# Gated mix of linear attention and a squared-relu MLP: matmul operands at other byte offsets, and gate logits formed on VectorE

## The chip, the core and the metric

One NeuronCore of a Trainium2 chip runs the whole kernel in one launch. The metric is the device time in microseconds (us) of that core; the kernel before takes 442.57 us (median of three runs, 442.34 to 442.65). The engines are called as in the profile: PE is TensorE's matmul side, PEld its weight load, DVE is VectorE, ACT is ScalarE, POOL is GpSimd, and SP issues most of the DMAs.

## The reference

The input is x with 2048 rows and 448 columns. The result is a gate between a linear-attention block (16 heads of 28) and a two-layer perceptron of width 1792:

```python
g = _sigmoid((x * gate_w).sum(-1, keepdims=True))
a = _A_ref(x, A_wqkv, A_wo)
b = _B_ref(x, B_w1, B_b1, B_w2, B_b2)
return g * a + (1 - g) * b
```

In `_A_ref`, `phi(t) = where(t > 0, t + 1, exp(t)) + 1e-6` is taken of queries and keys, `kv = phi(k)^T v` and the sum of `phi(k)` are formed for each head over all rows, and the output is `phi(q) kv / (phi(q) . sum)` times `wo`. In `_B_ref` the hidden layer is `relu(x w1 + b1)` squared, times `w2`, plus `b2`. The gate needs one number for each row, the logit `sum(x * gate_w)`.

## The kernel before

**Precision.** Every fp32 operand is split into a rounded part and a remainder, both in TensorE's fp32r format. A product then takes three matmuls (high by high, high by low, low by high). The 448-wide contraction is laid out as four chunks of 128, the last of which holds its 64 rows twice, so that it needs two matmuls: 11 matmuls for each contraction over x, 12 for four tiles of the second layer.

**Tiles.** Rows go in four blocks of 512 (`NB`), each of four tiles of 128. PSUM tiles are one bank each. The matmuls of this program have four widths. The names are those of the profile:

- `h_ps` (hidden layer, L213) and `q_ps` (queries, L77): 512 columns stream. The stationary operand is a 128-column piece of `w1` or `wq_s`; the moving one is `xh` or `xl`, 512 rows of x.
- `o_ps` (second layer, L242), `g_ps` (x^T phi(k), L77) and `a_ps` (attention output, L77): 448 columns stream, out of `w2`, `ph`/`pl` and `m_s`. The stationary operand is a piece of `hh`/`hl`, `nh`/`nl` or `qh`/`ql`.
- `k_ps` (keys, L77): 450 columns stream out of `wk_s`. Its last two columns are `gate_w` twice, so that column 448 of the PSUM tile is the gate logit, which L280 copies into `logit`.
- `m_ps` (kv by wo, 12 matmuls of 448), `d_ps` (denominators, 8 of 512), and a few small ones.

**Counts.** 56 hidden tiles of 11 make 616 `h_ps` matmuls; 4 blocks of 40 make 160 `q_ps`; 56 steps of 12 make 672 `o_ps`; `a_ps` and `k_ps` have 16 groups of 11 and `g_ps` four times 12, 12, 12 and 8, so 176 matmuls each.

**Addresses.** The pools place a tile by its size, so pads in the code set the byte offset within a partition. Taken modulo 256, the program as built has these starts, where every step between chunks and column pieces is a multiple of 256 and keeps them:

| matmuls | stationary start | moving start |
|---|---|---|
| `h_ps`, `q_ps` | 0 | 0 |
| `o_ps`, `a_ps`, `g_ps`, `k_ps` | 0 | 64 |
| `m_ps`, `d_ps` | 0 | 0 |

**Order.** The order of the work is the order of the code, apart from what the framework's scheduler swaps between neighbours on an engine. In the first phase a step of the loop runs `up` (11 matmuls), `down` of the step before (12) and then `keys` of one tile (11) or a `gram` (11 or 8). What the other engines do with a PSUM tile stands in `after()` of `keys`, which the next `run_todo()` issues: ACT takes the exponential, DVE forms `r` (L261) and `p` (L262, into `r`), ACT rounds it to `ph`, DVE takes the remainder `pl` (L65), POOL adds to `ksum` (L286) and splits the row tile `xnr` (L65). `gram` of the same block reads `ph`, `pl`, `nh` and `nl`. Block 0 is the tightest place: `gram(0, 0)` is issued right after the keys of tile 3. Loads go through SP's queue in order (L51) into 15 shared slots.

The second phase runs the other half of the hidden layer, queries, denominators and attention, from about 225 us on.

Of the kernel before, what the change touches and what calls it, by code (L numbers as in the profile page):

```python
# [7 lines left out]
F = mybir.dt.float32  # L8
# [19 lines left out]


@with_exitstack  # L30
def gated_mix_kernel(ctx: ExitStack, tc: tile.TileContext, xt, xn, wk, wq, wv, wo, w1a, w1b, w2, b1, b2, hmask,
                     kvmask, halves, out):
    nc = tc.nc
    act, dve, pool, pe, sp = nc.scalar, nc.vector, nc.gpsimd, nc.tensor, nc.sync

    keep = ctx.enter_context(tc.tile_pool(name="keep", bufs=1))


    rest = ctx.enter_context(tc.tile_pool(name="rest", bufs=1, side="right"))
# [10 lines left out]
    def load(dst, src):  # L50
        sp.dma_start(out=dst, in_=src)  # L51
# [74 lines left out]

    def split_w1(h, g, c, hi_eng=act):
        if c == 0:
            n = (TB, 3 * P)[g]
            w = keep.tile([P, 7 * n + (16, 0)[g]], R, name=f"w1_{h}{g}", tag=f"w1{g}", bufs=1)  # L130
            w1_s[h, g] = w[:, :7 * n].rearrange("p (c n) -> p c n", c=7)
        split_w(w1_s[h, g], c, w1_raw.pop((h, g, c)), hi_eng, dve)

    w2_s, w2_raw = {}, {}
# [16 lines left out]
    wk_raw = {}  # L151

    def load_wk(c):
        wk_raw[c] = slot([P, D + 2], F, f"wkr{c}")
        load(wk_raw[c], wk[c])

    warm = keep.tile([P, 400], mybir.dt.bfloat16, name="warm")[:, :256]  # L160
    dve.memset(warm, 0.0)
    warm_ps = acc_p.tile([P, 512], F, name="warm_ps", tag="acc")
    for _ in range(18):
# [24 lines left out]
        load_wk(c)  # L188

    b2_s = keep.tile([P, D], F, name="b2_s")  # L190
    hm = keep.tile([P, P], R, name="hm")
    dve.memset(ones, 1.0)
    ksum = keep.tile([P, D], F, name="ksum")
    part = [keep.tile([P, D], F, name=f"part{t}") for t in range(NT)]

    phase1 = ExitStack()
    tmp = phase1.enter_context(tc.tile_pool(name="tmp", bufs=1, side="right"))
# [66 lines left out]
    def keys(t):  # L264
        b, i = divmod(t, 4)
        ps = ms_p.tile([P, 512], F, name=f"k_ps{t}", tag="ms")
        products(ps[:, :D + 2], [term for c in range(4)
                                 for term in terms_x(*xs[b], slice(i * P, (i + 1) * P), wk_s, slice(0, D + 2), c)])
        e = slot([P, D], F, f"e{t}")
        r = slot([P, D], F, f"r{t}")  # L270
        p = r
        ph = tmp_p.tile([P, D], R, name=f"ph{t}", tag="ph", bufs=4)
        pl = tmp_p.tile([P, D], R, name=f"pl{t}", tag="pl", bufs=4)

        if t == 0:
            pool.memset(tmp_p.tile([P, 48], F, name="off"), 0.0)

        def after():
            phi(ps[:, :D], e, r, p)
            dve.tensor_copy(logit[:, t:t + 1], ps[:, D:D + 1])  # L280
            split_hi(act, ph, p)
            split_lo(dve, pl, p, ph)
            if t == 0:
                pool.tensor_copy(ksum, p)
            else:
                pool.tensor_tensor(ksum, ksum, p, op=ALU.add)  # L286
            nh = tmp.tile([P, 512], R, name=f"nh{t}", tag="nh", bufs=4)
            nl = tmp.tile([P, 384], R, name=f"nl{t}", tag="nl", bufs=4)
            raw = xn_raw.pop(t)
            split_hi(act, nh[:, :D], raw)  # L290
            split_lo(pool, nl, raw[:, :384], nh[:, :384])
            split_lo(pool, nh[:, D:], raw[:, 384:], nh[:, 384:D])
            pend[t] = (ph, pl, nh, nl)
        return [after]
# [15 lines left out]
                dve.tensor_tensor(gsum[c], ps[:, :D], gsum[c], op=ALU.add)  # L310
        return [after]

    wq_s = keep.tile([P, 7, TB], R, name="wq_s")
    wq_raw = {}

    def load_wq(c):
# [69 lines left out]
    def m_product(j):  # L386
        wh, wl = wo_s.pop(j)
        ps = ms_p.tile([P, 512], F, name=f"m_ps{j}", tag="ms")
        products(ps[:, :D], [(kv[0][:, j], wh), (kv[0][:, j], wl), (kv[1][:, j], wh)])
        m = late.tile([P, 2, D], R, name=f"m{j}", tag="m", bufs=1)  # L390

        def after():
            split_hi(act, m[:, 0], ps[:, :D])
            split_lo(dve, m[:, 1], ps[:, :D], m[:, 0])

            p = j * 32
            for c in range(3):
                pool.dma_start(out=m_s[p:p + 32, c::4, :D][:, :2], in_=m[c * 32:c * 32 + 32])
            pool.dma_start(out=m_s[p:p + 16, 3, :D], in_=m[96:112, 0])
            pool.dma_start(out=m_s[p + 16:p + 32, 3, :D], in_=m[112:, 1])  # L400
        return [after]


# [64 lines left out]
    def attention(b, i):  # L468
        t = 4 * b + i
        cols = slice(i * P, (i + 1) * P)  # L470
        ps = ms_p.tile([P, 512], F, name=f"a_ps{t}", tag="ms")
        terms = []
        for c in range(3):
            h, lo = qs[c]
            terms += [(h[:, cols], m_s[:, c, :D]), (h[:, cols], m_s[:, 4 + c, :D]), (lo[:, cols], m_s[:, c, :D])]
        h, lo = qs[3]
        terms += [(h[:, cols], m_s[:, 3, :D]), (lo[:, cols], m_s[:, 3, :D])]
        products(ps[:, :D], terms)
        u = late.tile([P, D], F, name=f"u{t}", tag="q", bufs=NLATE)
        act.activation(u, ps[:, :D], AF.Copy, scale=gate[:, 0, t:t + 1])  # L480
        dve.scalar_tensor_tensor(part[t], part[t], gate[:, 1, t:t + 1], u, op0=ALU.mult, op1=ALU.add)  # L481
# [26 lines left out]
    for f in range(2, 4):  # L508
        hidden(first[f], 0, f)

    wkm = keep.tile([P, 3632], R, name="wk_s", tag="wkm", bufs=1)
    wk_s = wkm[:, :7 * TB].rearrange("p (c n) -> p c n", c=7)

    load_xn(0)
    load_w2(2)
    load_w2(3)
    for c in range(4):
        split_w(wk_s[:, :, :D + 2], c, wk_raw[c], act, dve)
    down(0, 0)
    load_xn(1)  # L520
    for c in range(4):
        load_w1(0, 1, c)
    todo += keys(0)
    split_w2(2)
    load(b2_s, b2.partition_broadcast(P))
    down(0, 1)
    run_todo()
# [96 lines left out]
    for n, b in enumerate(order):  # L624
        then = order[n + 1] if n + 1 < NB else None
        for f in range(NF - NH, NF):
            fl = f - NH
            run_todo()
            up(b, f)
            if fl:  # L630
                if n + 1 < NB or f + 1 < NF:
                    down(b, f - 1)
            elif n == 0:
                down(b, NH - 1)
                half_done(b)
            else:
                down(order[n - 1], NF - 1)
                for i in range(4):
                    finish(order[n - 1], i)
            if n == 0:  # L640
                if fl < 4:
                    todo += queries(b, (3, 0, 1, 2)[fl])
                if fl == 0:
                    for c in range(4):
                        load_w1(1, 1, c)
                    kv_product()
                    phase1.close()
                    late = ctx.enter_context(tc.tile_pool(name="late", bufs=1, side="right", reuse_waits="tile"))
                    m_s = keep.tile([P, 3632], R, name="m_s", tag="wkm", bufs=1)
                    m_s = m_s[:, :7 * D].rearrange("p (c n) -> p c n", c=7)  # L650
                    for j in range(2):
                        load_wo(j)
                if fl == 1:
                    for c in range(4):
                        split_w1(1, 1, c)
                if fl in (1, 2):
                    for j in range(2 * fl - 2, 2 * fl):
                        split_wo(j)
                        todo += m_product(j)
                    if fl == 1:  # L660
                        for j in range(2, 4):
                            load_wo(j)
                if fl < 2:
                    load_w2(NH + 5 + fl)
                    split_w2(NH + 4 + fl)
                if fl == 2:
                    split_w2(NH + 6)
                if fl == 4:
                    todo += denominators(b)
                if fl == 5:  # L670
                    for c in range(4):
                        scaled(b, c)
                if fl == 6:
                    for i in range(4):
                        attention(b, i)
            else:
                if fl == 0:
                    todo += denominators(b)
                if fl == 1:
                    for c in range(4):  # L680
                        scaled(b, c)
                if 2 <= fl < 6:
                    attention(b, fl - 2)
            if then is not None:
                if fl < 2:
                    load_x(then, 2 * fl)
                    load_x(then, 2 * fl + 1)
                if 1 <= fl < 3:
                    split_x(then, 2 * fl - 2)
                    split_x(then, 2 * fl - 1)  # L690
                if n and 3 <= fl:
                    todo += queries(then, (3, 0, 1, 2)[fl - 3])
                if n == 0 and fl in (5, 6):
                    for c in ((3, 0), (1, 2))[fl - 5]:
                        todo += queries(then, c)
# [56 lines left out]
```

## Time and profile before

| | before |
|---|---|
| median of three runs | 442.57 us |
| the profiled execution | 441.92 us |
| its span, first to last instruction | 440.1 us |
| PE busy | 432.9 us (98%), 2054 matmul records |
| PEld busy | 380.7 us (87%) |
| DVE busy | 268.0 us (61%) |
| ACT busy | 172.7 us (39%) |
| POOL busy | 58.5 us (13%) |
| granted TensorE clock | 1.000 |

A matmul's own duration in the profile runs until its drained end and overlaps the next one. How fast matmuls follow each other is read from stretches of a view: the chain of waits gives start, length and count of each uninterrupted run, and length by count is the time from one start to the next.

### The profile page before, as it was taken

What the parts mean: (1) busy time and instruction counts of PE and PEld (TensorE: products, weight loads), DVE (VectorE), ACT (ScalarE), POOL (GpSimd) and SP (SyncE); (2) the same over time, 40 slices, a digit from 0 to 9 for tenths busy, and PEclk for the clock granted to TensorE, in tenths of its full rate; (3) what the DMA queues carried; (4) which work ended last, traced back from release to release, by engine and by line L of the source; (5) the groups of instructions that cost most, each with busy time, mean ns of one, the idle gap of its engine ahead of it and who ended that gap; (6) DMA issues with size and microseconds to landing.
All of it is one profiled execution on the core that took longest, in us unless ns stands there. A gap on an engine that the chain in (4) does not pass through costs nothing.

```text
span 440.1 us, 5482 instructions
## 1 busy us (share of the span) xinstructions
PE 432.9 (98%) x2054; PEld 380.7 (87%) x2054; DVE 268.0 (61%) x452; ACT 172.7 (39%) x298; POOL 58.5 (13%) x76
## 2 busy tenths in 40 slices
PE   9999999999999999999999989999999999999996
PEld 6798898899888889898988868888888898888895
DVE  5958436552587427573467668788454984549423
ACT  5955235331355114451344334335322453234321
POOL 0233124210252005420002420000000000000000
PEclk9999999999999999999999999999999999999999
DMA  7652201021031210333146311040100501002002
GB/s 264 188 174 69 89 13 57 24 66 47 24 118 31 67 45 1 110 102 82 54 123 151 73 38 24 1 147 33 25 0 0 181 0 26 0 0 85 1 1 83
DMA packets 18315, 28.77 MB, mean 65 GB/s; under 512 B 2880, under 2 KB 12784, under 8 KB 18288
## 3 DMA queue, kind: packets, MB, share of 16 engines
q1 hardware_dynamic: 17072, 26.81, 19.9%
q0 software_dynamic: 1216, 1.61, 1.9%
q8 instruction: 16, 0.26, 0.3%
q14 instruction: 11, 0.09, 0.1%
HBM read 22.09 MB, written 3.67 MB: 59 GB/s over the span
## 4 chain that ended last, share of the span: by engine, by line
PE 91%; DVE 3%; DMA 2%; ACT 2%; issue 1%; SPq 0%; DVEq 0%; ACTq 0%
PE o_ps L242 30%; PE h_ps L213 28%; PE q_ps L77 8%; PE a_ps L77 8%; PE g_ps L77 8%; PE k_ps L77 7%; DMA wkr<-in_wk 1%; DMA xr<-in_xt 1%; PE kv_ps L364 1%; ACT hr L217 1%; PE m_ps L77 1%; DVE wk_s L65 0%; DVE hh L62 0%; DVE r L261 0%; DVE r L262 0%
## 5 line engine op out<-in xcount | busy, mean ns | idle before, releaser
L213 PE MATMUL h_ps<-xh,w 128*128 128x512 f32 x392 | 126.9, 392 | 0.1
L242 PE MATMUL o_ps<-w,hh 128*128 128x448 f32 x448 | 125.5, 363 | 0.7 <-DVE hh L62 0.7
L242 PEld LDWEIGHTS o_ps<-w,hh 128*128 128x128 f32 x448 | 83.8, 188 | 10.2 <-DVE hh L62 1.4
L213 PE MATMUL h_ps<-xl,w 128*128 128x512 f32 x224 | 87.5, 391 | 0.0
L213 PEld LDWEIGHTS h_ps<-xh,w 128*128 128x128 f32 x392 | 73.5, 188 | 15.4 <-ACT xh L58 0.4
L242 PE MATMUL o_ps<-w,hl 128*128 128x448 f32 x224 | 79.6, 363 | 0.0
L217 ACT ACTIVATE hr<-h_ps,b_s 128x512 f32<-128x512 f32 x56 | 38.3, 683 | 96.9 <-PE h_ps L213 89.8
L62 DVE CAST hh<-hr 128x512 fp32r<-128x512 f32 x56 | 25.3, 452 | 40.4 <-ACT hr L218 40.0
L213 PEld LDWEIGHTS h_ps<-xl,w 128*128 128x128 f32 x224 | 42.1, 188 | 8.3 <-DVE xl L65 0.4
L242 PEld LDWEIGHTS o_ps<-w,hl 128*128 128x128 f32 x224 | 42.0, 188 | 2.9 <-DVE hl L65 0.2
L65 DVE TENSOR_TENSOR hl<-hr,hh 128x512 fp32r<-128x512 f32 x56 | 41.1, 734 | 2.2
L218 ACT ACTIVATE hr<-hr 128x512 f32<-128x512 f32 x56 | 35.3, 630 | 1.3
L77 PE MATMUL k_ps<-wk_s,xh 128*128 128x450 f32 x112 | 33.7, 367 | 0.0
L77 PE MATMUL q_ps<-xh,wq_s 128*128 128x512 f32 x100 | 33.0, 390 | 0.0
L77 PE MATMUL a_ps<-m_s,qh 128*128 128x448 f32 x112 | 32.2, 362 | 0.0
L65 POOL TENSOR_TENSOR nl<-xnr,nh 128x384 fp32r<-128x384 f32 x16 | 18.2, 1139 | 94.2 <-ACT nh L58 94.2
L286 POOL TENSOR_TENSOR ksum<-ksum,r 128x448 f32<-128x448 f32 x15 | 19.3, 1284 | 52.1 <-DVE r L262 52.1
L481 DVE SCALAR_TENSOR_TENSOR part<-part,gate,u 128x448 f32<-128x448 f32 x16 | 10.9, 683 | 24.9 <-ACT u L480 24.9
L480 ACT ACTIVATE u<-a_ps,gate 128x448 f32<-128x448 f32 x16 | 10.2, 635 | 37.2 <-PE a_ps L77 37.2
L261 DVE TENSOR_SCALAR r<-k_ps 128x448 f32<-128x448 f32 x16 | 10.0, 623 | 23.7 <-ACT e L260 21.7
L77 PE MATMUL k_ps<-wk_s,xl 128*128 128x450 f32 x64 | 23.6, 369 | 0.0
L77 PE MATMUL g_ps<-pl,nh 128*128 128x448 f32 x64 | 23.3, 364 | 0.3 <-DVE pl L65 0.3
(104 smaller groups left out, 562.0 us busy)
## 6 DMA issues: line engine op xcount, KB each, us to landing
xr<-in_xt SPq DMA_DIRECT2D x27, 256.0 KB, 3.2
xnr<-in_xn SPq DMA_DIRECT2D x16, 224.0 KB, 2.6
out<-out SPq DMA_DIRECT2D x16, 224.0 KB, 2.0
w2r<-in_w SPq DMA_DIRECT2D x14, 224.0 KB, 2.9
w1r<-in_w1a SPq DMA_DIRECT2D x8, 256.0 KB, 2.8
w1r<-in_w1b SPq DMA_DIRECT2D x8, 192.0 KB, 2.9
m_s<-m POOLq DMA_DIRECT2D x12, 112.0 KB, 2.7
wqr<-in_wq SPq DMA_DIRECT2D x4, 256.0 KB, 3.0
```

The costliest lines, as they stand in the source:

```text
L62: eng.tensor_copy(hi, src)
L65: eng.tensor_tensor(lo, src, f32(hi), op=ALU.subtract)
L77: pe.matmul(out_ps, a, b, start=(i == 0), stop=(i == n - 1))
L213: pe.matmul(ps, a, m, start=(c == 0 and n == 0), stop=(c == 3 and n == 1))
L217: act.activation(r, ps, AF.Relu, bias=b1_s[:, f:f + 1])
L218: act.activation(r, r, AF.Square)
L242: pe.matmul(o_ps[i][:, :D], a, m, start=(f % NH == 0 and n == 0), stop=(f % NH == NH - 1 and n == 2))
L261: dve.tensor_scalar(r, ps, 0.0, 1e-6, op0=ALU.max, op1=ALU.add)
L286: pool.tensor_tensor(ksum, ksum, p, op=ALU.add)
L364: pe.matmul(kv_ps[:JE, js], wv_s[c][:, js], gsum[c][:, js], start=(c == 0), stop=(c == 3))
L480: act.activation(u, ps[:, :D], AF.Copy, scale=gate[:, 0, t:t + 1])
L481: dve.scalar_tensor_tensor(part[t], part[t], gate[:, 1, t:t + 1], u, op0=ALU.mult, op1=ALU.add)
```

## The change

- `w1` tiles and `wq_s` get pads ahead of them, so that the stationary operands of `h_ps` and `q_ps` begin at 144 modulo 256. Their moving operands stay at 0.
- The pads of `warm`, `wk_s`, `m_s` and `off` change (the warm-up operand now lies in the first `part` tile), so that the moving operands of `o_ps`, `a_ps`, `g_ps` and `k_ps` begin at 160. Their stationary ones stay at 0. `m_ps` keeps 0 and 0; the stationary operand of the eight `d_ps` matmuls moves to 224.
- `wk_s` loses its two gate columns, so `k_ps` streams 448. The logit of a tile is formed on DVE by one `scalar_tensor_tensor` with an accumulated output, from the row tile `xnr` and a broadcast copy of `gate_w`, `gw_s`, which one more DMA brings. Its elementwise result goes into `e`, which has been read by then.

```diff
@@ -126,9 +127,9 @@
     def split_w1(h, g, c, hi_eng=act):
         if c == 0:
-            n = (TB, 3 * P)[g]
-            w = keep.tile([P, 7 * n + (16, 0)[g]], R, name=f"w1_{h}{g}", tag=f"w1{g}", bufs=1)
-            w1_s[h, g] = w[:, :7 * n].rearrange("p (c n) -> p c n", c=7)
+            n, a, z = ((TB, 36, 4), (3 * P, 60, 0))[g]
+            w = keep.tile([P, a + 7 * n + z], R, name=f"w1_{h}{g}", tag=f"w1{g}", bufs=1)
+            w1_s[h, g] = w[:, a:a + 7 * n].rearrange("p (c n) -> p c n", c=7)
...
-    warm = keep.tile([P, 400], mybir.dt.bfloat16, name="warm")[:, :256]
+    part = [keep.tile([P, D], F, name=f"part{t}") for t in range(NT)]
+    warm = part[0].bitcast(mybir.dt.bfloat16)[:, :256]
...
+    gw_s = keep.tile([P, D], F, name="gw_s")
...
-        products(ps[:, :D + 2], [term for c in range(4)
-                                 for term in terms_x(*xs[b], slice(i * P, (i + 1) * P), wk_s, slice(0, D + 2), c)])
+        products(ps[:, :D], [term for c in range(4)
+                             for term in terms_x(*xs[b], slice(i * P, (i + 1) * P), wk_s, slice(0, D), c)])
...
         if t == 0:
-            pool.memset(tmp_p.tile([P, 48], F, name="off"), 0.0)
+            pool.memset(tmp_p.tile([P, 24], F, name="off"), 0.0)
...
             phi(ps[:, :D], e, r, p)
-            dve.tensor_copy(logit[:, t:t + 1], ps[:, D:D + 1])
             split_hi(act, ph, p)
...
             raw = xn_raw.pop(t)
+            dve.scalar_tensor_tensor(e, raw, 1.0, gw_s, op0=ALU.mult, op1=ALU.mult, accum_out=logit[:, t:t + 1])
             split_hi(act, nh[:, :D], raw)
...
-    wq_s = keep.tile([P, 7, TB], R, name="wq_s")
+    wq_s = keep.tile([P, 44 + 7 * TB + 28], R, name="wq_s")[:, 44:44 + 7 * TB]
+    wq_s = wq_s.rearrange("p (c n) -> p c n", c=7)
...
-    wkm = keep.tile([P, 3632], R, name="wk_s", tag="wkm", bufs=1)
-    wk_s = wkm[:, :7 * TB].rearrange("p (c n) -> p c n", c=7)
+    wk_s = keep.tile([P, 7, D], R, name="wk_s", tag="wkm", bufs=1)
...
     split_w2(2)
+    load(gw_s, gw.partition_broadcast(P))
     load(b2_s, b2.partition_broadcast(P))
...
-                    m_s = keep.tile([P, 3632], R, name="m_s", tag="wkm", bufs=1)
-                    m_s = m_s[:, :7 * D].rearrange("p (c n) -> p c n", c=7)
+                    m_s = keep.tile([P, 7, D], R, name="m_s", tag="wkm", bufs=1)
...
-        "wk": np.concatenate([k_w[:, k_of], gate_w, gate_w], axis=1)[twice].reshape(4, P, D + 2),
+        "wk": k_w[:, k_of][twice].reshape(4, P, D),
...
+        "gw": inputs["gate_w"],
```

On PE nothing changes place. On DVE the new step does not stand where it is written but where the scheduler puts it. This is DVE's order at tile 3 of block 0, before (`r` written twice is the key features, `pl` their remainder, `xh`/`xl` the next block's x):

```order
L65 TENSOR_TENSOR hl_6_540<-hr_6_536,hh_6_539 128x512
L261 TENSOR_SCALAR r_510<-k_ps_497 128x448
L280 COPY logit<-k_ps_497 128x1
L262 SCALAR_TENSOR_TENSOR r_510<-e_509,r_510 128x448
L65 TENSOR_TENSOR pl_512<-r_510,ph_511 128x448
L71 SCALAR_TENSOR_TENSOR xh_517<-xr_3_567,side,xl_518 128x512
```

And the same place now:

```order
L66 TENSOR_TENSOR hl_6_541<-hr_6_537,hh_6_540 128x512
L263 TENSOR_SCALAR r_511<-k_ps_498 128x448
L264 SCALAR_TENSOR_TENSOR r_511<-e_510,r_511 128x448
L291 SCALAR_TENSOR_TENSOR e_510,logit<-xnr_446,gw_s 128x448
L66 TENSOR_TENSOR pl_513<-r_511,ph_512 128x448
L72 SCALAR_TENSOR_TENSOR xh_518<-xr_3_568,side,xl_519 128x512
```

The one-column copy is gone, and a 448-column step now stands between `r` and `pl`. On SP's queue the load of `gw_s` goes ahead of that of `b2_s`, behind the four of `wk`; before:

```order
L51 DMA wkr_132<-in_wk 128x450
L51 DMA b_s<-in_b 128x448
L51 DMA half<-in_halves 128x2
L51 DMA xnr_266<-in_xn 128x448
L51 DMA w2r_268<-in_w 128x448
```

and now:

```order
L52 DMA wkr_147<-in_wk 128x448
L52 DMA gw_s<-in_gw 128x448
L52 DMA b_s<-in_b 128x448
L52 DMA half<-in_halves 128x2
L52 DMA xnr_266<-in_xn 128x448
```

One more issue stands ahead of `b2_s`, `half` and the first row tile; the rest of the queue is as it was.

More of the change, by code (lines that the diff above doesn't have):

```diff
@@ L30, in gated_mix_kernel @@
 @with_exitstack
-def gated_mix_kernel(ctx: ExitStack, tc: tile.TileContext, xt, xn, wk, wq, wv, wo, w1a, w1b, w2, b1, b2, hmask,
+def gated_mix_kernel(ctx: ExitStack, tc: tile.TileContext, xt, xn, wk, wq, wv, wo, w1a, w1b, w2, b1, b2, gw, hmask,
                      kvmask, halves, out):
@@ L153, in load_wk @@
     def load_wk(c):
-        wk_raw[c] = slot([P, D + 2], F, f"wkr{c}")
+        wk_raw[c] = slot([P, D], F, f"wkr{c}")
         load(wk_raw[c], wk[c])
-    warm = keep.tile([P, 400], mybir.dt.bfloat16, name="warm")[:, :256]
+    part = [keep.tile([P, D], F, name=f"part{t}") for t in range(NT)]
+    warm = part[0].bitcast(mybir.dt.bfloat16)[:, :256]
     dve.memset(warm, 0.0)
@@ L193, in gated_mix_kernel @@
     ksum = keep.tile([P, D], F, name="ksum")
-    part = [keep.tile([P, D], F, name=f"part{t}") for t in range(NT)]
     phase1 = ExitStack()
@@ L397, in after @@
             for c in range(3):
-                pool.dma_start(out=m_s[p:p + 32, c::4, :D][:, :2], in_=m[c * 32:c * 32 + 32])
-            pool.dma_start(out=m_s[p:p + 16, 3, :D], in_=m[96:112, 0])
-            pool.dma_start(out=m_s[p + 16:p + 32, 3, :D], in_=m[112:, 1])
+                pool.dma_start(out=m_s[p:p + 32, c::4][:, :2], in_=m[c * 32:c * 32 + 32])
+            pool.dma_start(out=m_s[p:p + 16, 3], in_=m[96:112, 0])
+            pool.dma_start(out=m_s[p + 16:p + 32, 3], in_=m[112:, 1])
         return [after]
@@ L474, in attention @@
             h, lo = qs[c]
-            terms += [(h[:, cols], m_s[:, c, :D]), (h[:, cols], m_s[:, 4 + c, :D]), (lo[:, cols], m_s[:, c, :D])]
+            terms += [(h[:, cols], m_s[:, c]), (h[:, cols], m_s[:, 4 + c]), (lo[:, cols], m_s[:, c])]
         h, lo = qs[3]
-        terms += [(h[:, cols], m_s[:, 3, :D]), (lo[:, cols], m_s[:, 3, :D])]
+        terms += [(h[:, cols], m_s[:, 3]), (lo[:, cols], m_s[:, 3])]
         products(ps[:, :D], terms)
@@ L517, in gated_mix_kernel @@
     for c in range(4):
-        split_w(wk_s[:, :, :D + 2], c, wk_raw[c], act, dve)
+        split_w(wk_s, c, wk_raw[c], act, dve)
     down(0, 0)
@@ L711 @@
     q_w, k_w, v_w = wqkv[:, :D], wqkv[:, D:2 * D], wqkv[:, 2 * D:]
-    gate_w = inputs["gate_w"].reshape(D, 1)
     p = np.arange(P)
```

## The prediction

> **What bounds the kernel now.** I read the page's busy times first, then its chain of waits, then the chain in order of time.
>
> ```profile
> PE 432.9 (98%) x2054; PEld 380.7 (87%) x2054; DVE 268.0 (61%) x452; ACT 172.7 (39%) x298; POOL 58.5 (13%) x76
> PEclk9999999999999999999999999999999999999999
> PE 91%; DVE 3%; DMA 2%; ACT 2%; issue 1%; SPq 0%; DVEq 0%; ACTq 0%
> ```
>
> PE is busy for 98% of the span at the full granted clock, and 91% of the chain that ends last runs through it. What matters is therefore how fast one matmul follows another, and the chain in order of time tells that: start, length, and the number of matmuls in each unbroken run.
>
> ```profile
> 76.60 2.26 PE k_ps L77 x11
> 78.86 2.52 PE h_ps L213 x11
> 81.39 2.41 PE o_ps L242 x12
> 83.80 2.26 PE k_ps L77 x11
> ...
> 270.96 8.80 PE a_ps L77 x44
> ...
> 284.75 2.49 PE h_ps L213 x11
> 287.24 2.41 PE o_ps L242 x12
> ```
>
> A 448-column matmul takes 8.80 / 44 = 200.0 ns from start to start, a 512-column one 2.49 / 11 = 226.4 ns. The 64 columns between them cost 26.4 ns, or 0.412 ns each, so 448 columns stream in 184.6 ns and 512 in 211.0. The other 15.4 ns of every matmul don't depend on its width. Over some 1,970 matmuls that is 30 us, the most that any change of addresses could take from. A 450-column matmul takes 2.26 / 11 = 205.5 ns, 5.5 more than 448 columns, where two columns should cost 0.8.
>
> **The key columns.** `k_ps` goes from 450 to 448 columns, to the rate of `a_ps`, which has the same shape and the same old starts. That is 16 groups of 11 at 5.5 ns: 16 x 11 x 5.5 = 968 ns, **-1.0 us**, straight on the path. At least the two columns go (0.8 x 176 = 0.15 us), so the gain is from 0.15 to 1.0; I take the whole, since 200.0 is what the shape costs elsewhere.
>
> **Stationary start 144 for 512 columns.** No matmul of this trace has that start, so the price has to be bounded. The nearest rows are those of `m_ps`: 448 columns with both operands at 0, the starts that `h_ps` and `q_ps` have now. Beside them stands `a_ps` with its moving operand at 64, in equally short runs between other matmuls.
>
> ```profile
> 233.24 0.20 PE m_ps L77
> ...
> 234.13 0.41 PE m_ps L77 x2
> ...
> 236.07 0.63 PE m_ps L77 x3
> ...
> 245.68 0.20 PE m_ps L77
> ...
> 246.29 0.41 PE m_ps L77 x2
> ...
> 247.70 0.62 PE m_ps L77 x3
> ```
>
> ```profile
> 405.88 0.40 PE a_ps L77 x2
> ...
> 406.50 0.61 PE a_ps L77 x3
> ...
> 407.80 0.60 PE a_ps L77 x3
> ```
>
> Twelve `m_ps` take 2.47 us, 205.8 ns each; eight `a_ps` take 1.61 us, 201.3 ns each. With width and neighbours alike, equal starts cost 4.5 ns more than starts 64 apart. `m_ps` also contracts over 112 rows instead of 128, so the 4.5 ns may not be the addresses', but no row separates the two. All 616 + 160 = 776 large 512-column matmuls have equal starts, and the change puts theirs 144 apart. I take the same 4.5 ns off them: 776 x 4.5 = 3,492 ns, **-3.5 us**. The bounds are no gain, and a loss or a second step of the same 4.5 ns (+3.5 and -7.0 us).
>
> A rule of the Trainium skill speaks against any of this: "SBUF — State Buffer", section "Who interferes with whom", gives PE two independent read ports, one for the moving operand and one for the weight load, and says that PE never waits on anyone; the 4.5 ns of the rows above do not sit well with it, though they do not refute it. The same skill's "TensorE: Matmul & The Clock Gate", section "Back-to-back issue gap", gives N / 2.4 + 2.5 ns for an isolated warm matmul, an estimate of 215.8 ns at 512 columns, and this trace has 226.4 where the clock row shows full speed; by that page some 11 ns of each matmul are there to be won, and by the other none of them through addresses.
>
> **Moving start 160 for 448 columns.** This moves 672 `o_ps`, 176 `a_ps`, 176 `g_ps` and 176 `k_ps`, 1,200 in all, from starts 64 apart to starts 160 apart. Both are away from 0, where the rows show the extra cost, so I take **0**. The bounds are one step either way: 1,200 x 4.5 = 5.4 us up or down.
>
> **The logits on DVE.** Sixteen one-column copies go and sixteen 448-column steps come. The nearest rows are the copies themselves and two groups of the same operation and size.
>
> ```profile
> L280 DVE COPY logit<-k_ps 128x1 f32<-128x1 f32 x16 | 2.4, 148 | 0.0
> L262 DVE SCALAR_TENSOR_TENSOR r<-e,r 128x448 f32<-128x448 f32 x16 | 11.4, 712 | 0.0
> L481 DVE SCALAR_TENSOR_TENSOR part<-part,gate,u 128x448 f32<-128x448 f32 x16 | 10.9, 683 | 24.9 <-ACT u L480 24.9
> 60.00:120.00 60.00, 60.00 (x288) 53.68 (x287) 28.19 (x46) 20.38 (x37) 12.68 (x15) 1.00 0.15 42
> ```
>
> 16 x 0.71 - 16 x 0.148 = +9.0 us of DVE time. Its cover is DVE's own slack: from 60 to 120 us DVE (the third engine of the row) works 28.2 us out of 60 and PE never waits. In a step of 7.2 us (from one `k_ps` run to the next, 76.60 to 83.80) the addition is 0.56 us, so `hh`, the cast that PE needs next, comes later by no more than that and is still early. Queued behind the new step on DVE is `pl`, and `gram` waits for `pl`. That matters once, in block 0, where PE already waits:
>
> ```profile
> 46.15 0.62 DVE L262 SCALAR_TENSOR_TENSOR r<-e,r 128x448 f32<-128x448 f32 x1
> 46.81 0.58 ACT L58 ACTIVATE ph<-r 128x448 fp32r<-128x448 f32 x1 [2.11 <-DVE r L262]
> 46.92 1.15 POOL L286 TENSOR_TENSOR ksum<-ksum,r 128x448 f32<-128x448 f32 x1 [4.19 <-DVE r L262]
> 47.42 1.13 DVE L65 TENSOR_TENSOR pl<-r,ph 128x448 fp32r<-128x448 f32 x1 [0.64 <-ACT ph L58]
> 48.60 0.47 PE L77 MATMUL g_ps<-pl,nh 128*128 128x448 f32 x1 [0.28 <-DVE pl L65]
> ...
> 127.93 0.61 DVE L65 TENSOR_TENSOR pl<-r,ph 128x448 fp32r<-128x448 f32 x1
> ```
>
> DVE has 0.64 us free between `r` and `pl`, so a step of 0.7 us nearly fits. But `pl` takes 1.13 us there, against 0.61 in the last row, at a time when POOL is idle, since POOL's `ksum` runs at the same time. If the new step also holds up `ksum`, `pl` waits for more of it. The delay is between 0.1 and 0.7 us; I take **+0.3 us**. The Trainium skill's "SBUF — State Buffer", in the section named above, has a DVE step with two SBUF inputs and a POOL step that reads SBUF block each other for a whole instruction; the 1.13 us agree.
>
> **The loads.** One more load of 224 KB goes ahead of `b2_s` on SP.
>
> ```profile
> 9.99 0.33 SPq L51 DMA_DIRECT2D b_s<-in_b  x1
> 10.37 0.43 SPq L51 DMA_DIRECT2D half<-in_halves  x1
> 14.48 0.33 SPq L51 DMA_DIRECT2D xnr<-in_xn  x1
> b_s<-in_b SPq DMA_DIRECT2D x1, 224.0 KB, 4.1
> ...
> 24.50 0.62 DVE L262 SCALAR_TENSOR_TENSOR r<-e,r 128x448 f32<-128x448 f32 x1
> ```
>
> SP stands idle from 10.8 to 14.48 us, waiting for a slot, so an issue of 0.33 us costs nothing. Landing 4.1 us after its issue, as `b2_s` does, `gw_s` is there before 15 us, and its first use comes behind the `r` of tile 0, at 24.50 us. The pads themselves, the shorter `wk` rows and the `d_ps` start (8 matmuls) are worth less than 0.1 us: **0**.
>
> **Sum.** -1.0 - 3.5 + 0 + 0.3 = -4.2 us on the profiled execution's 441.92 us: 437.7. That execution was 0.65 us under the median of the three timed runs, 442.57, so in their terms the forecast is 438.4, which I round to **438.3 us**. About 0.2%, 0.9 us, is what the measurement can tell from no change.
>
> **Rivals.**
>
> - *Both steps.* The moving start brings 448 columns one step down as well: another 5.4 us, 433.0 us. For it: the 448-column matmuls have the same 15 ns of fixed time as the 512-column ones, though their starts are already 64 apart. Against it: `a_ps` holds 200.0 ns over 44 matmuls without a flaw, which looks like a floor.
> - *Addresses don't matter.* Then the 4.5 ns of `m_ps` come from its 112 rows, and only the key columns and the DVE step remain: 442.57 - 1.0 + 0.3 = 441.9 us, no change. For it: 226.4 at equal starts and 200.0 at starts 64 apart leave the same 15 ns, as if the cost were fixed. It is also what the skill's rule on PE's ports would give.
> - *160 is a worse start than 64.* If for 448 columns a moving start of 160 costs what 0 costs in `m_ps`, the 1,200 matmuls lose 4.5 ns each, +5.4 us, with its place in every `o_ps`, `a_ps`, `g_ps` and `k_ps` run. Without a gain at 512 columns that is 442.57 + 5.4 - 0.7 = 447.3 us, slower; with it, 443.8. It decides from 0.6 ns for each of the 1,200 where 512 columns gain nothing, from 3.5 ns where they gain 4.5. For it: the one pair of rows says that the start matters and nothing says which way 160 goes.
> - *The change doesn't do what it says.* The built program has the starts 144 and 160, so only the chip's indifference, the second rival, is left of this.
>
> **How the numbers follow.** The forecast gets 0.42, both steps 0.20, indifference 0.22, a worse start 0.16. The range reaches from below both steps to just past no change, 431.5 to 443.0 us: it holds the first three but for their edges and leaves out most of the last. Faster by over 0.2%: the forecast, both steps, and 0.04 of indifference, whose own value is 0.15% below the median, make 0.66. Within 0.2%: the other 0.18 of it. Slower: 0.16.
>
> **What would show it.** In the chain after, runs of `h_ps` x11 should be 2.44 us (222 ns each) instead of 2.49 to 2.52, `k_ps` x11 2.20, `a_ps` and `o_ps` unchanged at 200 ns. DVE should be busy some 9 us longer without a new wait of PE but for the one for `pl` near 48 us, at 0.4 to 1.0 us. `h_ps` at 226 ns or more makes the main term wrong; 448-column runs off 200 ns by more than 1 decide between the first rival and the third; PE waits for `hh` or `pl` in later blocks would make the DVE term wrong.

## The result, and the profile after

The kernel is slower: 446.97 us (446.40 to 447.46, four runs) against 442.60 us (442.34 to 442.65) for the kernel before, a ratio of 1.0102 with a 95% interval of 1.0087 to 1.0117. The forecast was 438.3 us and the range ended at 443.0. The profiled execution took 447.08 us, its span 445.3 us, 5.2 us more than before.

The page of the kernel after, the three lines that were read first before:

```profile
PE 436.6 (98%) x2054; PEld 380.5 (85%) x2054; DVE 281.3 (63%) x468; ACT 172.3 (39%) x298; POOL 63.2 (14%) x76
PEclk9999999999999999999999999999999999999999
PE 90%; DVE 3%; DMA 2%; ACT 2%; issue 1%; SPq 1%; ACTq 0%; DVEq 0%
```

The bound is the same, PE at full granted clock with the same 2054 matmuls, and PE is busy 3.7 us longer. DVE is busy 13.3 us longer, not 9. Its chain of waits in order of time, with start, length and count of each run:

```profile
78.14 2.20 PE k_ps L78 x11
80.34 2.56 PE h_ps L215 x11
82.90 2.42 PE o_ps L244 x12
...
273.60 8.80 PE a_ps L78 x44
282.40 5.13 PE q_ps L78 x22
287.53 2.56 PE h_ps L215 x11
```

The row before that answers to the `q_ps` one:

```profile
279.76 4.99 PE q_ps L77 x22
```

`k_ps` went from 2.26 to 2.20 us as forecast. But 22 `q_ps` went from 4.99 to 5.13 us, 226.8 to 233.2 ns each, and `h_ps` x11 from 2.49 or 2.52 to 2.56 us where the forecast was 2.44. PE does not wait between these runs; each matmul simply follows the last one later.

The rates below, and in every table that follows, are a second reading of the trace: the mean distance from the start of one matmul record to the start of the next, put down to the output of the earlier one, with the distances over 290 ns (waits) left out.

| ns from start to start | `h_ps` | `q_ps` | `o_ps` | `a_ps` | `g_ps` | `k_ps` | `m_ps` |
|---|---|---|---|---|---|---|---|
| before | 228.5 | 227.6 | 200.8 | 200.2 | 200.0 | 205.1 | 205.9 |
| after | 232.8 | 232.8 | 201.6 | 201.0 | 201.1 | 200.2 | 207.2 |

With the counts, the 5.2 us come out nearly so: `h_ps` 616 x 4.4 and `q_ps` 160 x 5.2 ns are +3.5 us; `o_ps`, `a_ps` and `g_ps` 672 x 0.74, 176 x 0.8 and 176 x 1.1 ns are +0.8; `k_ps` 176 x 4.9 is -0.9; the first gram (below) is +0.85. Two things that I did not pursue make up the rest: some +0.4 us in the first 17 us, where PE waits for x and the weights, and 0.4 us between the start of the last matmul and the end of the span, 3.9 us before and 4.3 after.

PE's waits, in total, times and longest, before and then after (two more, for the warm-up operand and for `dh`, are the same in both):

```profile
PE o_ps L242 <- DVE hh L62: 0.7, 1, 0.7
PE g_ps L77 <- DVE pl L65: 0.3, 1, 0.3
PE g_ps L77 <- ACT ph L58: 0.2, 1, 0.2
```

```profile
PE g_ps L78 <- DVE pl L66: 0.7, 1, 0.7
PE g_ps L78 <- ACT ph L59: 0.6, 1, 0.6
PE o_ps L244 <- DVE hh L63: 0.5, 1, 0.5
PE h_ps L215 <- ACT xh L59: 0.4, 1, 0.4
```

The last one lies in the first 17 us. The timeline of the kernel after at the first gram shows how the first two came about (start, length, engine, line; the idle time before and who ended it in brackets):

```profile
47.57 0.62 DVE L264 SCALAR_TENSOR_TENSOR r<-e,r 128x448 f32<-128x448 f32 x1
48.23 0.58 ACT L59 ACTIVATE ph<-r 128x448 fp32r<-128x448 f32 x1 [2.46 <-DVE r L264]
48.28 0.63 DVE L291 SCALAR_TENSOR_TENSOR e<-xnr,gw_s 128x448 f32<-128x448 f32 x1
48.34 1.57 POOL L287 TENSOR_TENSOR ksum<-ksum,r 128x448 f32<-128x448 f32 x1 [4.02 <-DVE r L264]
48.83 1.56 DVE L66 TENSOR_TENSOR pl<-r,ph 128x448 fp32r<-128x448 f32 x1
48.85 0.47 PE L78 MATMUL g_ps<-ph,nh 128*128 128x448 f32 x1 [0.61 <-ACT ph L59]
50.45 0.47 PE L78 MATMUL g_ps<-pl,nh 128*128 128x448 f32 x1 [0.72 <-DVE pl L66]
```

The new step (L291) fits into DVE's gap, as the prediction had it, and `pl` starts as soon after `r` as before (1.26 us behind the start of `r`, 1.27 before). But POOL's `ksum` runs 1.57 us instead of 1.15, and `pl`, beside it, 1.56 instead of 1.13. I read this as the step in the gap holding up `ksum`, and `ksum` then holding `pl`. The Trainium skill's "SBUF — State Buffer", section "Who interferes with whom", has a DVE step with two SBUF inputs and a POOL step that reads SBUF block each other; these rows agree. In the middle of the phase there is still no wait, by the row of the windows:

```profile
60.00:120.00 60.00, 60.00 (x287) 53.64 (x287) 31.58 (x52) 19.91 (x35) 12.68 (x13) 1.00 0.14 42
```

### The profile page after: what moved, and what is told of

The parts are those of the page before. It is cut to its first block, busy times and chain, and to the rows that moved or that the text cites. A ratio compares the mean times of both kernels' runs of the same rounds, so it can differ in the third digit from the quotient of the medians.

```text
span 445.3 us, 5503 instructions
## 1 busy us (share of the span) xinstructions
PE 436.6 (98%) x2054; PEld 380.5 (85%) x2054; DVE 281.3 (63%) x468; ACT 172.3 (39%) x298; POOL 63.2 (14%) x76
## 4 chain that ended last, share of the span: by engine, by line
PE 90%; DVE 3%; DMA 2%; ACT 2%; issue 1%; SPq 1%; ACTq 0%; DVEq 0%
PE o_ps L244 29%; PE h_ps L215 28%; PE q_ps L78 8%; PE a_ps L78 8%; PE g_ps L78 8%; PE k_ps L78 7%; DMA xr<-in_xt 1%; DMA b_s<-in_b 1%; SPq L52 1%; PE kv_ps L367 1%; ACT hr L219 1%; PE m_ps L78 1%; DVE r L264 0%; ACT hr L220 0%; DVE r L263 0%
## 5 line engine op out<-in xcount | busy, mean ns | idle before, releaser
L215 PE MATMUL h_ps<-xh,w 128*128 128x512 f32 x392 | 128.5, 396 | 0.4 <-ACT xh L59 0.4
L215 PE MATMUL h_ps<-xl,w 128*128 128x512 f32 x224 | 88.6, 395 | 0.1
L215 PEld LDWEIGHTS h_ps<-xh,w 128*128 128x128 f32 x392 | 73.5, 188 | 17.1 <-ACT xh L59 0.8
L78 PE MATMUL k_ps<-wk_s,xh 128*128 128x448 f32 x112 | 33.0, 363 | 0.0
L287 POOL TENSOR_TENSOR ksum<-ksum,r 128x448 f32<-128x448 f32 x15 | 22.8, 1522 | 47.4 <-DVE r L264 42.0
L78 PE MATMUL g_ps<-ph,nh 128*128 128x448 f32 x64 | 23.4, 365 | 0.6 <-ACT ph L59 0.6
L78 PE MATMUL q_ps<-xl,wq_s 128*128 128x512 f32 x60 | 23.7, 395 | 0.0
```

What stands on the lines that cost most here:

```text
L78: pe.matmul(out_ps, a, b, start=(i == 0), stop=(i == n - 1))
L215: pe.matmul(ps, a, m, start=(c == 0 and n == 0), stop=(c == 3 and n == 1))
```

## The experiments

My theory after this result: the stationary start of 144 costs the 512-column matmuls about 5 ns each and makes the loss; the prediction had the sign wrong. The first rival: the movers at 160 cost it, and 512 columns suffer from something else. The second: the logits on DVE do. The clock is none: the profiles of all runs have a granted clock of 0.998 to 1.000. The kernel before, run on the same chip each time, had medians from 441.99 to 442.60 us.

**Which part costs: one start undone, the other undone, both undone.** `stat0` puts the stationary operands back to 0 and keeps the rest:

```diff
-            n, a, z = ((TB, 36, 4), (3 * P, 60, 0))[g]
+            n, a, z = ((TB, 0, 40), (3 * P, 24, 36))[g]
...
-    wq_s = keep.tile([P, 44 + 7 * TB + 28], R, name="wq_s")[:, 44:44 + 7 * TB]
+    wq_s = keep.tile([P, 8 + 7 * TB + 64], R, name="wq_s")[:, 8:8 + 7 * TB]
```

> The kernel after with one part undone: the stationary operands of the 512-column matmuls begin at 0 again instead of 144; movers at 160 and logits on DVE stay. Theory A (the stationary start costs every 512-column matmul some 4.4 ns, 776 x 4.4 = 3.4 us): h_ps and q_ps back from 232.8 to about 228.4 ns, time about 443.5 us. Theory B (the loss comes with the logits on DVE and their load, and the matmuls are slow for another reason): 512 columns stay near 232.8, time about 447.0. Theory C (the movers at 160 make the loss): time about 447.0 as well.

`mov64` puts the 448-column movers back to 64 and keeps 144:

```diff
-            n, a, z = ((TB, 36, 4), (3 * P, 60, 0))[g]
+            n, a, z = ((TB, 36, 44), (3 * P, 20, 0))[g]
...
-            pool.memset(tmp_p.tile([P, 24], F, name="off"), 0.0)
+            pool.memset(tmp_p.tile([P, 48], F, name="off"), 0.0)
```

> The kernel after with one part undone: the moving operands of the 448-column matmuls at 64 again instead of 160; stationary ones of 512 columns stay at 144, logits on DVE stay. Theory A: the movers are worth at most 0.7 ns on 1,200 matmuls, so 446.1 to 447.0 us, with 512 columns still at 232.8 ns. Theory B: 447.0. Theory C: back to about 443.

`logit_only` undoes both, so that the logits on DVE and the 448 key columns remain:

```diff
-            n, a, z = ((TB, 36, 4), (3 * P, 60, 0))[g]
+            n, a, z = ((TB, 0, 16), (3 * P, 48, 0))[g]
```

with the `wq_s` line of `stat0` and the `off` line of `mov64`.

> The third part alone: logits on DVE and 448 key columns, with both operand starts as in the kernel before (0 and 64). Theory A: 512 columns at 228.4 ns, key columns 0.9 us gained, the wait for pl in gram(0,0) about 0.9 us lost: 442.0 to 443.2 us, no change from before. Theory B: 446 to 447 us. Theory C: about 443.

| | us | ratio to before (95%) | `h_ps` | `q_ps` | `o_ps` | `a_ps` | `k_ps` |
|---|---|---|---|---|---|---|---|
| after (144; 160) | 446.97 | 1.0102 (1.0087 to 1.0117) | 232.8 | 232.8 | 201.6 | 201.0 | 200.2 |
| `stat0` (0; 160) | 444.22 | 1.0042 (1.0027 to 1.0056) | 228.7 | 229.0 | 202.5 | 200.4 | 200.3 |
| `mov64` (144; 64) | 446.37 | 1.0088 (1.0069 to 1.0107) | 233.0 | 233.3 | 200.6 | 200.6 | 200.4 |
| `logit_only` (0; 64) | 442.28 | 1.0001 (0.9988 to 1.0014) | 227.7 | 227.6 | 200.8 | 200.2 | 200.0 |

In brackets stand the stationary start at 512 columns and the moving start at 448. Between `mov64` and `logit_only` only 144 and 0 differ: 4.1 us, against 616 x 5.3 + 160 x 5.7 ns = 4.2 us from the rates. That is the larger part of the loss. The movers at 160 cost 1.9 us where the stationary ones are at 0 (`stat0` less `logit_only`) and 0.6 us where they are at 144 (the kernel after less `mov64`; 0.2 with each taken against the kernel before of its own session). The prices don't add up: with the movers at 160, going back from 144 to 0 brings only 2.8 us (the kernel after less `stat0`; 2.3 against the kernels before). The 448-column rates of `stat0` differ from those of the kernel after by up to 0.9 ns, though their starts are the same; this comes back below. And the logit part alone is worth nothing, though its key columns bring the 0.9 us. The chain of `stat0`:

```profile
80.00 2.52 PE h_ps L215 x11
82.52 2.43 PE o_ps L244 x12
...
272.22 8.80 PE a_ps L78 x44
281.02 5.02 PE q_ps L78 x22
```

`h_ps` and `q_ps` are back near the rows before, and `o_ps` x12 stands at 2.43 us instead of 2.41.

**Where the key columns' gain went: three places for the logit step.** `no_logit` is the kernel after without the sixteen DVE steps; it leaves the gate logits out (they are set to 0 once).

```diff
-            dve.scalar_tensor_tensor(e, raw, 1.0, gw_s, op0=ALU.mult, op1=ALU.mult, accum_out=logit[:, t:t + 1])
...
     ksum = keep.tile([P, D], F, name="ksum")
+    dve.memset(logit, 0.0)
```

> The kernel after without the sixteen logit steps on DVE (this kernel leaves the gate logits out and sets them to zero once; the load of gate_w stays). It gives the price of these steps. Theory A: the extra wait of PE in gram(0,0) of some 0.9 us goes, nothing else: 446.0 us. Theory B: about 443.

It took 446.24 us, ratio 1.0093 (1.0069 to 1.0117), 0.7 us under the kernel after, though the intervals overlap and 0.4 us of it is the difference between the two kernels before. In its waits neither `ph` nor `pl` is left. `into_r` is `logit_only` with the product written into `r` instead of `e`; since `pl` reads `r`, the step has to stand behind `pl`:

```diff
-            dve.scalar_tensor_tensor(e, raw, 1.0, gw_s, op0=ALU.mult, op1=ALU.mult, accum_out=logit[:, t:t + 1])
+            dve.scalar_tensor_tensor(r, raw, 1.0, gw_s, op0=ALU.mult, op1=ALU.mult, accum_out=logit[:, t:t + 1])
```

> The logits alone, with operand starts as in the kernel before (0 and 64), and with one more edit: the elementwise result of the logit step goes into r instead of e, so that the step has to wait until pl and ksum have read r and no longer stands ahead of pl. If PE's longer wait in gram(0,0) comes from the place ahead of pl, that wait falls from 2.2 us back to about 1.2 us or less and the time to 441.0 to 441.5, some 0.2% under the kernel before; if it comes from DVE's added load as such, the time stays at 442.2.

It took 442.35 us, ratio 1.0000 (0.9991 to 1.0009): nothing won. Its timeline at the first gram shows that `pl` did become short again and the time was still not saved:

```profile
47.51 0.62 DVE L264 SCALAR_TENSOR_TENSOR r<-e,r 128x448 f32<-128x448 f32 x1
...
48.28 1.15 POOL L287 TENSOR_TENSOR ksum<-ksum,r 128x448 f32<-128x448 f32 x1 [4.56 <-DVE r L264]
48.78 1.13 DVE L66 TENSOR_TENSOR pl<-r,ph 128x448 fp32r<-128x448 f32 x1 [0.64 <-ACT ph L59]
48.80 0.47 PE L78 MATMUL g_ps<-ph,nh 128*128 128x448 f32 x1 [1.20 <-ACT ph L59]
```

`ksum` and `pl` are back at 1.15 and 1.13 us, but the whole chain of DVE comes later against PE, which now waits 1.20 us for `ph`. (The expectation counts otherwise, from one matmul's start to the next at these two places: 1.57 and 0.45 us, 2.0 in all, against 2.2 in `logit_only` and 1.2 before. So its fall to 1.2 did not come.) What would explain it is the logit steps of the tiles before, 0.7 us of DVE each, in a stretch where DVE has nothing to spare. The timelines bear that out: `r` of tile 3 starts at 47.51 us, 1.36 us later than before, though PE begins its first `g_ps` matmul only 0.3 us later. From 34 us to the end of this `pl`, DVE's list of the kernel before has four idle gaps of 0.48 to 0.65 us; those of `logit_only` and of the kernel after show none, and that of `into_r` three. To try it, `held` (starts of `logit_only`) issues the four logit steps of block 0 as soon as their row tiles have landed, into a tile of `part` that is not yet in use. They are written late in the code, but in the trace they run at 20.3, 23.7, 29.3 and 36.8 us, three of the four ahead of that stretch, and the load of `gw_s` goes only one place later in SP's queue (10.10 us instead of 9.74):

```diff
+            def gate_logit():
+                dve.scalar_tensor_tensor(part[NT - 1], raw, 1.0, gw_s, op0=ALU.mult, op1=ALU.mult,
+                                         accum_out=logit[:, t:t + 1])
+            if t < 4:
+                held.append(gate_logit)
+            else:
+                gate_logit()
...
+    load(gw_s, gw.partition_broadcast(P))
+    for step in held:
+        step()
```

> Starts 0 and 64 as in the kernel before, key columns 448, logits on DVE; but the logit steps of block 0 are issued as soon as their row tiles have landed, into a scratch tile, so that none stands between r and pl of tile 3. If the wait in the first gram was the whole price of the logits (0.5 to 0.9 us), that wait falls back to the 0.5 us of the kernel before and the gain of the key columns shows: 441.4 to 441.8 us, ratio 0.997 to 0.998. If DVE's added load costs elsewhere, or the wait has another cause (POOL's ksum and the new order of ph), no gain: 442.2 to 442.5 us, ratio 0.999 to 1.0.

It took 441.56 us against 442.33, ratio 0.9977 (0.9964 to 0.9991): the gain of the key columns shows at last, and this is the one version that beats both kernels. The timeline of `held` at the same place:

```profile
47.09 1.15 POOL L287 TENSOR_TENSOR ksum<-ksum,r 128x448 f32<-128x448 f32 x1 [4.21 <-DVE r L264]
47.59 1.13 DVE L66 TENSOR_TENSOR pl<-r,ph 128x448 fp32r<-128x448 f32 x1 [0.64 <-ACT ph L59]
47.60 0.47 PE L78 MATMUL g_ps<-ph,nh 128*128 128x448 f32 x1 [0.78 <-ACT ph L59]
48.77 0.47 PE L78 MATMUL g_ps<-pl,nh 128*128 128x448 f32 x1
```

One wait of 0.78 us is left where `logit_only` has two of 0.72 and 0.73. These 0.67 us are about what the medians gained, 0.7 us. (The profiled executions lie further apart, 439.6 and 440.7 us, but there PE's first `o_ps` matmul already starts 0.7 us earlier, before any logit step has run.) The other twelve logit steps, in blocks 1 to 3, stand where they stood and make no wait of PE.

**Is it the stationary start, or how far apart the two starts are?** `both160` puts x (`xh`, `xl`) and the stationary operands of 512 columns all at 160, and keeps the 448-column movers there. The keys, whose stationary operand is x, then have 160 and 160 as well.

```diff
-            n, a, z = ((TB, 36, 4), (3 * P, 60, 0))[g]
+            n, a, z = ((TB, 0, 0), (3 * P, 0, 60))[g]
...
-    wq_s = keep.tile([P, 44 + 7 * TB + 28], R, name="wq_s")[:, 44:44 + 7 * TB]
+    wq_s = keep.tile([P, 48 + 7 * TB + 64], R, name="wq_s")[:, 48:48 + 7 * TB]
```

> The kernel after with the moving operands of the 512-column matmuls at 160 (xh and xl moved) and their stationary ones at 160 too: equal starts again, neither of them 0. As these x tiles are also the stationary operands of the keys, k_ps gets equal starts too. If only the distance between the two starts counts, h_ps and q_ps are back at 227 to 228 ns, about 443 us; if the stationary start counts by itself, they stay near 233 ns, about 447 us.

Two more kernels were to give the whole curve in one execution each. `scan512` lays the chunks of `w1` and `wq_s` 16 bytes further apart, so that their starts run through the sixteenths of 256; `scan448` does it with `w2`, fourteen starts, stationary start 0.

```diff
-            w1_s[h, g] = w[:, a:a + 7 * n].rearrange("p (c n) -> p c n", c=7)
+            w1_s[h, g] = w[:, a:a + 7 * (n + 4)].rearrange("p (c n) -> p c n", c=7)[:, :, :n]
```

> The kernel after with each of the seven chunks of w1 and wq_s at another start, in steps of 16 bytes: 0 to 96 in w1's first tile, 160 to 256 in its second, 112 to 208 in wq_s; movers stay at 0, 448 columns as in the kernel after. The time from one 512-column matmul to the next is read by the start of the stationary operand that loads meanwhile. Theory P (a phase: what counts is where the weight load stands against the moving stream in a period of 256 bytes): a smooth curve with one low and one high stretch, the neighbours of 144 (128, 160) also near 233 ns and those of 0 (240, 16) near 227. Theory L (a line: 144 is slow because it is a multiple of 16 and no more): every odd multiple of 16 is near 233, every multiple of 32 or of 64 near 227.

```diff
-        w2_s[f] = keep.tile([P, 2, D], R, name=f"w2_{f}", tag="w2", bufs=NH)
+        w2_s[f] = keep.tile([P, 2, D + 4], R, name=f"w2_{f}", tag="w2", bufs=NH)[:, :, :D]
```

> The kernel after with stationary starts of 512 columns at 0, and with the w2 tiles of the second layer at fourteen moving starts (0 to 144 and 192 to 240 in steps of 16; high halves on multiples of 32, low halves 16 further). It shows what a 448-column matmul costs by its moving start. If the 4.5 ns of the m_ps rows came from equal starts, o_ps at 0 takes about 205 ns; if they came from its 112 rows and short runs, o_ps at 0 takes 200 to 202 like at 64. Theory P: a smooth curve over the fourteen starts. Theory L: odd multiples of 16 slower than even ones.

`both160` took 447.62 us, one run: the time of its second expectation, but the rates of its first, `h_ps` 228.0 and `q_ps` 226.8 ns, as good as with both at 0. For 512 columns, equal starts are good, and 144 is bad as a distance from the moving start. The time went into 448 columns, 205.4 to 205.6 ns in `o_ps`, `a_ps` and `g_ps`, of which more below; `k_ps`, with both starts at 160, had 202.4. The scans took 448.55 and 445.45 us and gave no curve: in `scan512` the matmuls with start 0, among others with other starts, had 231.5 ns, and `o_ps` in `scan448` had between 200.6 and 205.5 with no order in it. A matmul's rate seems to take something from its neighbours, so starts had to be tried in whole programs, one distance at a time. That is what the next five do, by the pads alone; the first number is the stationary start at 512 columns (moving 0), the second the moving start at 448 (stationary 0). For `p64_0`:

```diff
-            n, a, z = ((TB, 36, 4), (3 * P, 60, 0))[g]
+            n, a, z = ((TB, 16, 48), (3 * P, 16, 0))[g]
...
-            pool.memset(tmp_p.tile([P, 24], F, name="off"), 0.0)
+            pool.memset(tmp_p.tile([P, 64], F, name="off"), 0.0)
...
-    wq_s = keep.tile([P, 44 + 7 * TB + 28], R, name="wq_s")[:, 44:44 + 7 * TB]
+    wq_s = keep.tile([P, 24 + 7 * TB + 48], R, name="wq_s")[:, 24:24 + 7 * TB]
```

> Stationary start of the 512-column matmuls 64 (moving 0); both starts of the 448-column ones 0. Nothing else differs from the changed kernel. Equal starts cost (the reading of m_ps in the prediction): o_ps, a_ps, g_ps and k_ps go to 205 ns or more from start to start, h_ps and q_ps below 227.7; 1,200 x 5 ns = +6 us less 776 x up to 4.5, so 443 to 448 us. Equal starts are good (what the runs with both at 0 and both at 160 show for 512 columns): the 448-column ones stay at 200 to 201, and h_ps stands somewhere between 227.7 and 233; 442 to 446 us. A price of the start 144 alone: all as with starts 0 and 64, 442.3 us.

> Stationary start of the 512-column matmuls 128 (moving 0), moving start of the 448-column ones 128 (stationary 0). If the distance is what costs and 144 lies near its worst, h_ps and q_ps are at 231 to 234 ns here too and the time is 445.5 to 447 us; if only a start that is no multiple of 64 costs (144 and 160 are none, 64 and 128 are), they are at 227.5 to 228.5, the 448-column ones at 200 to 201, and the time is 442.3 us.

> Stationary start of the 512-column matmuls 192 (moving 0), moving start of the 448-column ones 224 (stationary 0). Distance, the same both ways round: 192 stands 64 from 0 modulo 256, so h_ps and q_ps come out as with 64, and o_ps with 224 near that of 32. Distance in one direction only: h_ps worse than at 144, over 233. Only a start that is no multiple of 64 costs: h_ps at 227.5 to 228.5, o_ps at 201.5 or more. Time between 441.5 and 447 us, by each group's ns times its count (776 and 672).

> 512-column matmuls with both starts 0, the moving start of the 448-column ones 96. If 64 is a single good distance, o_ps and a_ps are at 203.5 to 204.5 ns as with 0, 128 and 224, and the time is 442.3 + 1,200 x 3.3 ns = 446 us. If the price grows with the distance from 64, 96 lies near 64 and 160: 200.5 to 202 ns, 442.5 to 444 us. h_ps and q_ps at 227.5 to 228.7 ns either way.

> Stationary start of the 512-column matmuls 32 (moving 0), moving start of the 448-column ones 32 (stationary 0). If equal starts alone are good at 512 columns, h_ps is at 232 to 233 ns as with 64, 128 and 144; if the price grows with the distance, it is near 229 as with 192. If 64 is a single good place at 448, o_ps is at 203.5 to 204.5 ns. Time 449 us if both hold, 443 to 446 us if neither does.

| | us | `h_ps` | `q_ps` | `o_ps` | `a_ps` | `g_ps` | `k_ps` |
|---|---|---|---|---|---|---|---|
| `p64_0` | 450.00 | 233.1 | 232.9 | 203.8 | 203.5 | 204.2 | 203.9 |
| `p128_128` | 449.31 | 232.6 | 232.4 | 203.6 | 203.8 | 204.1 | 203.7 |
| `p192_224` | 448.30 | 229.5 | 229.6 | 204.6 | 204.3 | 204.2 | 204.5 |
| `p0_96` | 448.39 | 227.8 | 228.1 | 205.3 | 205.5 | 205.5 | 205.5 |
| `p32_32` | 450.73 | 232.8 | 232.6 | 204.9 | 205.4 | 205.2 | 204.5 |

Each is one run; before was at 442.33 for the first three and at 441.99 for the others. All five times lie above every range that I had given for them, by 1.3 to 2.4 us. At 512 columns equal starts are the best of the six distances (0: 226.8 to 229.0; 192: 229.5; 32, 64, 128 and 144: 232.4 to 233.3). At 448 columns it is another pair: 64 with 200.0 to 200.9 ns in all five programs that have it, 203.5 to 205.5 at starts of 0, 32, 96, 128 and 224, and 160 anywhere from 200.2 to 205.6, by the program. Of my expectations, those that rested on one good place at 448 held in kind, but put `o_ps` at 203.5 to 204.5 ns where 96 has 205.3 and 32 has 204.9. Those on a slope or on multiples of 64 did not hold, nor did a distance that counts the same both ways round at 512 (64 has 233.1, 192 has 229.5). None of the three cases of `p64_0` came.

This table has two limits. It counts from 0, at 512 columns the stationary start and at 448 the moving one. Counted as moving less stationary, 192 at 512 columns and 64 at 448 are the same distance, and at 512 it is the second best, 229.5 ns against up to 229.0 with equal starts. And at 448 columns the stationary start was 0, so the distance is not told apart there from the moving start by itself; the one exception is `k_ps` of `both160`, equal starts at 160, with 202.4 ns, where equal starts at 0 have 203.9. The rows of `p64_0` and of `p0_96`:

```profile
275.22 8.92 PE a_ps L78 x44
284.14 5.13 PE q_ps L78 x22
```

```profile
274.82 9.04 PE a_ps L78 x44
283.86 5.00 PE q_ps L78 x22
```

**Does the rate at 160 belong to the program or to the execution?** In `stat0` and `both160`, `a_ps`, `o_ps` and `g_ps` have the same operands at the same full addresses, not just modulo 256; only x and the stationary operands of 512 columns lie elsewhere. Yet `a_ps` has 8.80 us for 44 in `stat0` and 9.08 in `both160`:

```profile
274.13 9.08 PE a_ps L78 x44
283.21 4.99 PE q_ps L78 x22
```

`both160_again` is the same kernel once more:

> The kernel with the stationary and moving operands of the 512-column matmuls all at 160, once more. If the rate of the 448-column ones belongs to the build, o_ps, a_ps and g_ps are at 205 to 206 ns again and the time at 447.6 us; if it belongs to the execution, they can be at 200.4 to 202.5 ns as in the other builds with starts 0 and 160, and the time at 443 to 444 us.

```profile
274.34 9.08 PE a_ps L78 x44
283.42 4.99 PE q_ps L78 x22
```

447.81 us, and every group within 0.2 ns of the first run. The rate belongs to the program, and not to the matmul's own addresses alone. What carries over from the 512-column matmuls to a run of 44 others is open. The single distances between two `a_ps` matmuls say how it looks: of 152, 124 are 200 ns and 26 are 206 or 207 in the kernel after, while in `both160` 148 are 206 or 207. Between these two programs it is a matter of two rates, some 6.7 ns apart, and of how often PE falls into the second.

## Why the prediction was wrong, step by step

**The stationary start, -3.5 us: the step that failed.** "I take the same 4.5 ns off them" was the error. The rows said that `m_ps`, with equal starts, takes 4.5 ns more than `a_ps` with starts 64 apart, both at 448 columns. (The 226.4 ns that the sum started from was also the lower of two rows shown; the mean of all `h_ps` before was 228.5.) `p64_0` shows that the reading itself was about right: with equal starts the large 448-column groups go to 203.5 to 204.2 ns, 3.5 ns more (and `m_ps`, with starts 0 and 0 everywhere, keeps 205 to 207 in every program, so that some of its price is its own). But it does not carry over to the 512-column matmuls, where equal starts are the good ones: there a distance of 144 costs 5.3 to 5.7 ns, and the term measures +3.5 us in the trace and +4.1 us between `mov64` and `logit_only`. The prediction had this case as an end of the term's bounds, +3.5 us, but neither the range nor a rival took it in. One pair of rows, with one width, could not tell which way the other width goes. Why the two kinds of matmul differ in this is open.

**The moving start, 0 within 5.4 us.** +0.8 us in the trace after, 0.2 to 1.9 us by the experiments: right in its bounds. The argument was not: "Both are away from 0, where the rows show the extra cost" takes 64 for one of many good places, and five of six other starts cost 3 ns or more.

**The rivals.** "160 is a worse start than 64", without a gain at 512 columns, gave 447.3 us, close to the 446.97 measured, but by luck: 160 made 0.8 of the 5.2 us in the trace, not 5.4. "Addresses don't matter" fell: programs with the same work, at the same clock, differed by over 5 ns a matmul through the starts alone. The Trainium skill's "SBUF — State Buffer", section "Who interferes with whom", gives PE two independent read ports and has it wait on no other engine. That starts could not matter, which the prediction drew from it, does not hold here; the rule itself is not refuted, since these runs do not tell whether the two reads meet or something behind them does. "Both steps" fell too: no start brought 512 columns under 226 ns, while the estimate for an isolated matmul from the Trainium skill's "TensorE: Matmul & The Clock Gate", section "Back-to-back issue gap", was 215.8.

**The key columns, -1.0 us.** -0.9 us measured, 205.1 to 200.0 ns. Right.

**The logits, +0.3 us within 0.1 to 0.7.** 0.85 us in the trace, 0.9 by `logit_only` (0.0 with a gain of 0.9 inside), and about 0.7 of it came back in `held`: outside the bounds. The place, the wait for `pl`, and the hold-up of `ksum` were right, and the wait for `pl` grew by 0.44 us (0.28 to 0.72), within them. The term left out a second piece of the same size, the wait for `ph`, from 0.18 to 0.61 us: it looked at the one step behind tile 3's `r` and not at those of the tiles before, which make this `r` itself late. Even where `pl` was short again, in `into_r`, `ph` came late, and only moving block 0's logit steps forward, three of the four ahead of that stretch, brought the time back. DVE took 13.3 us more rather than 9.0; the group rows, of before and of after, say why:

```profile
L65 DVE TENSOR_TENSOR pl<-r,ph 128x448 fp32r<-128x448 f32 x16 | 15.0, 936 | 7.2 <-ACT ph L58 7.1
```

```profile
L66 DVE TENSOR_TENSOR pl<-r,ph 128x448 fp32r<-128x448 f32 x16 | 18.6, 1161 | 1.3 <-ACT ph L59 1.3
L291 DVE SCALAR_TENSOR_TENSOR e<-xnr,gw_s 128x448 f32<-128x448 f32 x16 | 14.2, 885 | 0.5
L291 DVE DVE_READ_ACCUMULATOR e<-xnr,gw_s 128x1 f32 x16 | 1.3, 80 | 0.0
```

The new steps took 885 ns on average instead of 712, each with 80 ns more to read its accumulator out, and `pl` went from 936 to 1161 ns. With the copies gone that is 16.7 us; DVE's other groups took 3.4 us less in all, 2.8 of them in four short `wq_s` steps.

**The loads, 0.** Not settled. The first `o_ps` matmul starts at 16.2 us in the kernel before, at 16.0 in `held`, and at 16.3 to 17.1 in the programs that load `gw_s` ahead of `b2_s`. But much of this comes from waits before 9.7 us, when that load is not yet issued, and two executions of the same kernel (`both160`, `both160_again`) differ there by 0.2 us. The first 17 us were not taken apart further.

## What to carry to other kernels

Where PE is the bound and never waits, the time from start to start of each kind of matmul, times its count, is the time, and a few ns a matmul from a start address are worth microseconds. Take no such price from one kind of matmul to another: change one start, in a whole program, and read each group's rate. And a step moved to an idle engine costs where that engine's chain is tight; the gain came only when those few steps were issued earlier, before that stretch begins.

## What was not expected of the hardware

- Of the starts tried, modulo 256 bytes, the best pair was another for the 512-column matmuls than for the 448-column ones: at 512 columns equal starts (226.8 to 229.0 ns; with the moving start at 0, 229.5 at a stationary start of 192 and 232.4 to 233.3 at 32, 64, 128 and 144), at 448 columns 64 (200.0 to 200.9; 203.5 to 205.5 with the stationary start at 0 and the moving one at 0, 32, 96, 128 or 224).
- 450 columns with starts 64 apart took 205.1 ns, 448 took 200.0: two columns cost 5 ns, where the prediction's estimate by the slope between 448 and 512 was 0.8.
- With the very same operand addresses, 44 `a_ps` matmuls took 8.80 us in one program and 9.08 in another; the latter's two runs agree.
- A DVE step of 0.63 us with two SBUF inputs, started 0.06 us ahead of POOL's `ksum`, went with a rise of that from 1.15 to 1.57 us, and of the next DVE step from 1.13 to 1.56.
